# Summing seven groups' diagonal output quadrants in DRAM with accumulating DMAs instead of in SBUF with GpSimd additions

## The chip, the cores and the metric

The kernel runs on one core of one Trainium2 chip. The metric is the device time of one execution in microseconds (us). The engines are PE (matmuls, with weight loads listed as PEld), DVE (VectorE), ACT (ScalarE), POOL (GpSimd) and SP, which mostly issues DMAs; POOL and ACT can issue DMAs too.

## The reference

Linear attention is followed by a mixture of eight experts with dense routing. The first part makes `x`, 4608 rows of 512. Then, with `P` a 4608 x 8 table from a few rounds of row and column normalisation:

```
out = zeros((N, D))                  # 4608 x 512, float32
for e in range(E):                   # 8 experts
    h = maximum(x @ w1[e], 0)        # 4608 x 1024
    ye = h @ w2[e]                   # 4608 x 512
    out += P[:, e:e+1] * ye
```

The change concerns the last line alone: where the weighted contributions of the experts are added up.

## The kernel before

The 4608 rows are nine groups of 512: groups 0 to 7 are the first 512 tokens of the eight batches, group 8 collects the remaining 64 tokens of each. A running sum `acc[g]` of 128 partitions x 4 row tiles x 512 columns, float32, lies in SBUF for every group and is stored to `out` when expert 7 has been added.

After the attention and the routing, the experts 1 to 7 run as a long stream of matmuls. The up projection works on pairs of groups (0,1), (2,3), (4,5), (6,7), two halves (`fp`) for each pair, and on group 8 alone; in each of these nine steps the down projection of one earlier group is interleaved. Expert 7 takes group 8 first. Both projections are block products with seven instead of eight half-size products (a Strassen-Winograd scheme), and two of the up projection's products for a pair are split once more in the same way (`chain`, line 1487). The scheme needs sums of blocks: sums of the weights (`sums_up`, `sums_down`), of hidden blocks (`S[0]` to `S[2]` in `down7`), all made by `sub` on DVE (line 1223), and sums inside PSUM (line 1499, `ps<-ps,U`). The copies and relus of the up projection lie on ACT (lines 1455, 1459, 1467) and DVE (line 1462).

An output group falls into four quadrants (i, j): i is one half of its four row tiles, j is one half of its 512 columns. The down products `Z2`, `X2` and `X4` give the off-diagonal quadrants; `read` adds them to `acc` with two DVE instructions (line 1656). The products `Y1`, for quadrant (0,0), and `Z1` and `X3`, both for (1,1), give the diagonal ones by `read2`: two ACT instructions scale the PSUM bank by `P` into a buffer `u` (line 1668, seen as `hx<-ps,P` in the profile), and one POOL addition adds `u` to `acc` (line 1671). `u` comes from a ring `V` of two buffers. So there are three POOL additions for each group and expert from expert 1 on.

The weights of the next expert are loaded by POOL's DMA queue (`load_w`, line 500). From expert 2 on, the load names `("acc", 4, 0, 0)` among what it reads, so that it is held back until the running sum of group 4's first quadrant has last been written. Block sums of `x` come from DRAM on SP's queue (`load_x`, lines 1333 and 1341, tiles `XI` and `X`), in rings of two and three buffers that PE frees.

Nothing of the order is written by hand from instruction to instruction. A planner (`Plan`) takes every operation with a modelled duration, a queue, its reads and writes and its ring buffers, and runs a greedy list schedule: of all operations that are ready, the one that can start first goes first, and of equals the one that was emitted first. Each engine and queue then gets its instructions in the order of that schedule and executes them in that order. So taking away or adding an operation can change the order on every engine. POOL additions and DVE's `sub` are marked as shared: the planner lets only one of them run at a time.

Of the kernel before, what the change touches and what calls it, by code (L numbers as in the profile page):

```python
# [12 lines left out]
ALU = mybir.AluOpType  # L13
# [101 lines left out]

class Op:
    __slots__ = ("eng", "dur", "lat", "nbytes", "fn", "left", "ready", "users", "idx", "end",
                 "bufs", "deps", "shared", "turn", "unit", "stop", "tiled", "ins", "behind")

    def after(self, user):  # L120

# [77 lines left out]
class Plan:  # L199
# [9 lines left out]
    def op(self, eng, dur, lat, fn, r=(), w=(), takes=(), nbytes=0, shared=False):  # L209


        o = Op()
        o.eng, o.dur, o.lat, o.fn, o.nbytes = eng, dur, lat, fn, nbytes
        o.users, o.idx, o.end, o.ready = [], len(self.ops) + self.prio, None, 0.0
        o.shared, o.turn, o.unit, o.tiled = shared, False, 0, 0
        o.ins = o.behind = None
        deps = {}
        for key in r:
            for d in self.last.get(key, ()):
                deps[id(d)] = d  # L220
        for key in w:
            for d in list(self.last.get(key, ())) + self.readers.get(key, []):
                deps[id(d)] = d
        bufs = list(takes)
        for key in list(r) + list(w):
            b = key[0] if isinstance(key, tuple) else key
            if isinstance(b, Buf):
                bufs.append(b)
        o.bufs = list({id(b): b for b in bufs}.values())
        for b in o.bufs:  # L230
            b.left += 1
        for key in r:
            self.readers.setdefault(key, []).append(o)
        for key in w:
            self.last[key] = [o]
            self.readers[key] = []
        o.deps = list(deps.values())
        o.left = len(o.deps)
        for d in o.deps:
            d.users.append(o)  # L240
        self.ops.append(o)
        return o
# [81 lines left out]
    def run(self, tc):  # L324
        done = self.schedule()
        with tc.manual_schedule():
            for o in done:
                o.ins = o.fn()
                if o.behind:
                    tc.add_manual_dep(  # L330
                        o.ins.ins, o.behind.ins.ins.name, mybir.DependencyInfo(
                            mybir.DependencyClass.Sync, mybir.DependencyReason.DATA),
                        reason="order at the shared port")
# [3 lines left out]
def kernel(  # L337
# [151 lines left out]
    def new(tag):  # L489
        return R[tag].new()  # L490
# [914 lines left out]
    def up7(A, gs, fp, X, H, r0):  # L1405
# [155 lines left out]
            steps.update(chain("s1", w, A["s4"][1] + r0, hb, [("banks", 0, 0)], keep))  # L1561
        return steps

    def acc_part(g, i, j):
        return lambda: acc[g][:, 2 * i:2 * i + 2, 256 * j:256 * j + 256]

# [29 lines left out]
    def down7(e, g, H, B7):  # L1596


        def a(i, j):
            return lambda k: H[k // 2]()[:, j, k % 2, 256 * i:256 * i + 256]  # L1600

        def hk(i, j, fps=(0, 1)):
            return [(H[fp], q, j, i) for fp in fps for q in range(2)]

        late, seen = akey(g), set()
        S = [new(f"S{i}") for i in range(3)]
        for fp in range(2):
            def h(i, j, fp=fp):
                return lambda: H[fp]()[:, j, :, 256 * i:256 * i + 256]

            def s(n, fp=fp):
                return lambda: S[n]()[:, 2 * fp:2 * fp + 2]

            f = (fp,)
            end0 = ["dn0"] if e == 1 else []
            sub(dve, 512, s(0), h(1, 0), h(1, 1), ALU.add, hk(1, 0, f) + hk(1, 1, f) + end0,
                [(S[0], fp)])
            sub(dve, 512, h(1, 0), h(0, 0), h(1, 0), ALU.subtract, hk(0, 0, f), hk(1, 0, f))
            sub(dve, 512, s(1), s(0), h(0, 0), ALU.subtract,
                [(S[0], fp)] + hk(0, 0, f), [(S[1], fp)])  # L1620
            sub(dve, 512, s(2), h(0, 1), s(1), ALU.subtract,
                [(S[1], fp)] + hk(0, 1, f), [(S[2], fp)])

        def sk(n):
            return [(S[n], fp) for fp in range(2)]

        def sa(n):
            return lambda k: S[n]()[:, k, :]

        def prod(bank, lhs, y, r, first, more=(), wk=()):  # L1630
            f, r2 = B7[y]
            product(bank, lambda k, i: lhs(k)[:, 128 * i:128 * i + 128],
                    lambda k: f()[:, k, :], 4, r + r2 + (["P"] if e else late) + list(more), first,
                    wk=wk)

        def start(bank, i, j):

            out_ = acc_part(g, i, j)
            w = [("acc", g, 2 * i + n, j) for n in range(2)]
            if (i, j) in seen:  # L1640
                dve(515, lambda: nc.vector.tensor_tensor(
                    out=out_(), in0=bank().rearrange("p (a b) -> p a b", a=2), in1=out_(),
                    op=ALU.add), [bank] + late, w)
            else:
                act(512, lambda: nc.scalar.copy(
                    out=out_(), in_=bank().rearrange("p (a b) -> p a b", a=2)),
                    [bank] + late, w)
            seen.add((i, j))

        def read(bank, i, j):  # L1650

            if e == 0:
                return start(bank, i, j)
            for n in range(2):
                ts = 2 * i + n
                dve(320, lambda n=n, ts=ts: nc.vector.scalar_tensor_tensor(  # L1656
                    out=acc[g][:, ts, 256 * j:256 * j + 256],
                    in0=bank()[:, 256 * n:256 * n + 256], scalar=P[:, 4 * g + ts, e:e + 1],
                    in1=acc[g][:, ts, 256 * j:256 * j + 256], op0=ALU.mult, op1=ALU.add),
                    [bank, "P"], [("acc", g, ts, j)])  # L1660

        def read2(bank, i, j):

            if e == 0:
                return start(bank, i, j)
            u = new("V")
            for n in range(2):
                act(370, lambda n=n: nc.scalar.activation(  # L1668
                    out=u()[:, n, :], in_=bank()[:, 256 * n:256 * n + 256], func=ACT.Copy,
                    bias=0.0, scale=P[:, 4 * g + 2 * i + n, e:e + 1]), [bank, "P"], [(u, n)])  # L1670
            pool(695, lambda: nc.gpsimd.tensor_tensor(  # L1671
                out=acc[g][:, 2 * i:2 * i + 2, 256 * j:256 * j + 256],
                in0=acc[g][:, 2 * i:2 * i + 2, 256 * j:256 * j + 256], in1=u(), op=ALU.add),
                [(u, 0), (u, 1)], [("acc", g, 2 * i + n, j) for n in range(2)])

        if e == 1 and g < 9:
            for ts in range(4):
                act(670, lambda ts=ts: nc.scalar.activation(
                    out=acc[g][:, ts, :], in_=acc[g][:, ts, :], func=ACT.Copy, bias=0.0,
                    scale=P[:, 4 * g + ts, 0:1]), ["P", ("acc", g, ts), (H[0], 0, 1, 1)] + akey(g),  # L1680
                    [("acc", g, ts, j) for j in range(2)])
        x, y, z = new("P1"), new("PO"), new("P1")

        def X1():
            prod(x, a(0, 0), "11", hk(0, 0), True, sk(1) + hk(1, 0),
                 [("D", e, g)])
            act(512, lambda: nc.scalar.copy(out=y(), in_=x()), [x], [y])

        def Y1():
            prod(y, a(0, 1), "21", hk(0, 1), False, [("D", e, g)])  # L1690
            read2(y, 0, 0)

        def Z1():
            prod(z, sa(0), "t1", sk(0), True)
            read2(z, 1, 1)

        def X2():
            prod(x, sa(1), "t2", sk(1), False)
            read(x, 0, 1)

        def X3():
            prod(x, a(1, 0), "t3", hk(1, 0), False)
            read2(x, 1, 1)

        def Z2():
            prod(z, sa(2), "22", sk(2), False)
            read(z, 0, 1)

        def X4():
            prod(x, a(1, 1), "t4", hk(1, 1), False)  # L1710
            read(x, 1, 0)

        def stores():
            if e == E - 1 and g < 8:
                for ts in range(4):
                    store(g, ts)
            elif e == E - 1:
                held.extend(range(4))

        return {"out": stores, "X1": X1, "Y1": Y1, "Z1": Z1, "X2": X2, "X3": X3, "Z2": Z2, "X4": X4}  # L1720


# [26 lines left out]
    early, dn = [plain(8)], plain(7)  # L1749
    pairs = [(g, g + 1) for g in range(0, 8, 2)]  # L1750
    for e in range(1, E):
        w1, w2 = load_w(e, ["late", ("acc", 4, 0, 0)] if e > 1 else ["late"])
        if e == 1:
            nextX = sums_x(pairs[0])
# [67 lines left out]
```

## Time and the profile before

| what | value |
|---|---|
| time, three runs | 1013.84, 1014.08, 1014.84 us; median 1014.08 |
| span of the profiled execution | 1011.7 us |
| median less span (what lies around it) | 2.4 us |
| PE busy | 996.5 us, 99% |
| DVE, ACT, POOL busy | 84%, 79%, 38% |
| POOL additions of line 1671 | 186, 236.0 us in all |
| granted clock | 1.0 throughout |

Busy time of an engine counts its instructions as the profiler saw them. The chain that ended last follows the work back from the last instruction, at each step to what released it. A DMA's time to landing runs from its issue to the arrival of its data. The profiled execution's time is not listed apart from its span; the 2.4 us are the difference between the median and the span.

### The profile page before, as it was taken

What the parts mean: (1) busy time and instruction counts of PE and PEld (TensorE: products, weight loads), DVE (VectorE), ACT (ScalarE), POOL (GpSimd) and SP (SyncE); (2) the same over time, 40 slices, a digit from 0 to 9 for tenths busy, and PEclk for the clock granted to TensorE, in tenths of its full rate; (3) what the DMA queues carried; (4) which work ended last, traced back from release to release, by engine and by line L of the source; (5) the groups of instructions that cost most, each with busy time, mean ns of one, the idle gap of its engine ahead of it and who ended that gap; (6) DMA issues with size and microseconds to landing.
All of it is one profiled execution on the core that took longest, in us unless ns stands there. A gap on an engine that the chain in (4) does not pass through costs nothing.

```text
span 1011.7 us, 22473 instructions
## 1 busy us (share of the span) xinstructions
PE 996.5 (99%) x8195; PEld 713.6 (71%) x8232; DVE 851.8 (84%) x1979; ACT 797.0 (79%) x1786; POOL 379.7 (38%) x418
## 2 busy tenths in 40 slices
PE   7899999999999999999999999999999999999998
PEld 5666666644566867787777777787778777787775
DVE  8999989986888988789788988898778978888775
ACT  8999999836888787777777777768776877777774
POOL 5778764400133323342333323332333333433333
PEclk9999999999999999999999999999999999999999
DMA  9999989150114411171116121341126111612443
GB/s 253 198 191 177 166 148 134 38 115 1 48 48 96 114 48 48 48 138 56 48 48 117 48 57 52 73 93 48 48 51 144 48 48 48 110 53 69 154 154 142
DMA packets 115087, 93.94 MB, mean 93 GB/s; under 512 B 54432, under 2 KB 97440, under 8 KB 114976
## 3 DMA queue, kind: packets, MB, share of 16 engines
q1 hardware_dynamic: 83024, 68.46, 26.4%
q0 software_dynamic: 31648, 23.86, 17.0%
q8 instruction: 64, 1.05, 0.5%
q14 instruction: 47, 0.39, 0.1%
q10 hardware_dynamic: 304, 0.20, 0.1%
HBM read 92.62 MB, written 14.55 MB: 106 GB/s over the span
## 4 chain that ended last, share of the span: by engine, by line
PE 93%; ACT 3%; DVE 1%; DMA 1%; issue 1%; DVEq 0%
PE ps L1391 42%; PE ps L1400 25%; PE ps L605 17%; PE ps L1487 7%; PE ps L888 2%; ACT k L601 1%; ACT q L601 1%; DMA xT<-wx 1%; DVE wx L597 0%; PE ps L735 0%; DMA acc<-in_k_dram 0%; ACT wx L601 0%; PE ps L917 0%; ACT kr L601 0%; DVE m L597 0%
## 5 line engine op out<-in xcount | busy, mean ns | idle before, releaser
L1671 POOL TENSOR_TENSOR acc<-acc,hx 128x512 f32<-128x512 f32 x186 | 236.0, 1269 | 555.0 <-ACT hx L1668 287.5
L1391 PEld LDWEIGHTS <-hs 128*128 128x128 bf16 x1984 | 194.1, 98 | 56.2 <-issue 0.4
L1462 DVE CUSTOM_DVE_ANT_0 hs<-ps,U 128x512 bf16<-128x512 f32 x252 | 167.0, 685 | 46.6 <-PE ps L1400 29.0
L1668 ACT ACTIVATE hx<-ps,P 128x256 f32<-128x256 f32 x372 | 161.2, 482 | 45.2 <-PE ps L1391 42.3
L1467 ACT ACTIVATE hs<-ps 128x512 bf16<-128x512 f32 x252 | 151.1, 609 | 52.6 <-PE ps L1400 45.8
L1656 DVE SCALAR_TENSOR_TENSOR acc<-ps,P,acc 128x256 f32<-128x256 f32 x372 | 163.2, 476 | 31.8 <-PE ps L1391 30.7
L1391 PEld LDWEIGHTS <-hx 128*128 128x128 bf16 x1488 | 145.5, 98 | 27.1 <-issue 0.6
L1459 ACT COPY ps<-ps 128x512 f32<-128x512 f32 x252 | 146.4, 597 | 12.5 <-PE ps L1487 6.0
L1391 PE MATMUL ps<-hx,hs 128*128 128x256 bf16 x992 | 142.4, 273 | 0.1
L1400 PE MATMUL ps<-X,T 128*128 128x512 bf16 x448 | 131.5, 379 | 0.1
L1499 DVE TENSOR_TENSOR ps<-ps,U 128x256 f32<-128x256 f32 x192 | 75.5, 426 | 36.1 <-PE ps L1487 27.0
L1400 PEld LDWEIGHTS <-T 128*128 128x128 bf16 x672 | 65.7, 98 | 47.1 <-issue 0.6
L1455 ACT COPY U<-ps 128x512 f32<-128x512 f32 x126 | 74.7, 593 | 14.2 <-PE ps L1487 12.8
L1391 PE MATMUL ps<-wx,hs 128*128 128x256 bf16 x560 | 81.5, 273 | 0.0
L1391 PE MATMUL ps<-wx,hx 128*128 128x256 bf16 x496 | 75.9, 273 | 0.0
L1391 PE MATMUL ps<-hx 128*128 128x256 bf16 x496 | 75.9, 273 | 0.0
L1400 PE MATMUL ps<-xT,T 128*128 128x512 bf16 x224 | 72.5, 379 | 0.0
L605 PE MATMUL ps<-xT,w 128*128 128x512 bf16 x271 | 70.1, 379 | 0.6
L605 PE MATMUL ps<-w,hx 128*128 128x512 bf16 x274 | 69.7, 379 | 0.5
L1391 PE MATMUL ps<-w,hx 128*128 128x256 bf16 x432 | 69.8, 273 | 0.0
L1391 PE MATMUL ps<-w,hs 128*128 128x256 bf16 x432 | 64.7, 273 | 0.0
L597 DVE TENSOR_REDUCE m<-ps 128x4 f32<-128x512 f32 x88 | 58.7, 679 | 3.2 <-ACT k L601 1.5
(168 smaller groups left out, 1934.4 us busy)
## 6 DMA issues: line engine op xcount, KB each, us to landing
X<-xd SPq DMA_DIRECT2D x72, 256.0 KB, 2.7
wx<-in_moe_w_dram POOLq DMA_DIRECT2D x8, 1024.0 KB, 12.4
v_m<-in_v_dram SPq DMA_DIRECT2D x15, 512.0 KB, 5.7
out_dram<-acc SPq DMA_DIRECT2D x14, 512.0 KB, 3.2
w<-in_moe_w_dram POOLq DMA_DIRECT2D x6, 1024.0 KB, 10.8
XI<-xd SPq DMA_DIRECT2D x24, 192.0 KB, 2.5
qk<-in_k_dram POOLq DMA_DIRECT2D x12, 256.0 KB, 5.7
qk<-in_q_dram POOLq DMA_DIRECT2D x12, 256.0 KB, 6.9
```

What stands on the lines that cost most here:

```text
L605: nc.tensor.matmul(out_, lhsT=lhsT, rhs=rhs, start=start, stop=stop)
L1391: pe(256, lambda i=i, k=k, z=z: nc.tensor.matmul(bank()[:, 256 * i:256 * i + 256], lhsT=lhs(k, i), rhs=rhs(k), start=first and z, stop=k = ...
L1400: pe(512, lambda k=k: nc.tensor.matmul(bank().rearrange("p (a b) -> p a b", a=2), lhsT=lhs(k), rhs=rhs(k), start=first and k == 0, stop=k ...
L1455: act(512, lambda: nc.scalar.copy(out=u[q]().rearrange("p a b -> p (a b)"), in_=w[q]()), bk(w[q]), [u[q]])
L1459: act(512, lambda: nc.scalar.copy(out=to[q](), in_=x[q]()), bk(x[q]), [to[q]])
L1462: dve(515, lambda: nc.vector._custom_dve(ADD_SAT, out=out_(q, i, j), in0=bank[q]().rearrange("p (a b) -> p a b", a=2), in1=u[q](), s0=3.0e ...
L1467: act(512, lambda: nc.scalar.activation(out=out_(q, i, j), in_=bank[q]().rearrange("p (a b) -> p a b", a=2), func=ACT.Relu, bias=0.0, scal ...
L1487: pe(256, lambda: nc.tensor.matmul(at(i, h)(), lhsT=blocks[lhs]()[:, fp], rhs=rhs(), start=start, stop=True, skip_group_check=True), [*xal ...
L1499: dve(256, lambda: nc.vector.tensor_tensor(out=at(i, h)(), in0=at(1, 0)(), in1=s(), op=ALU.add), [k[1, 0], (p5, n)], [k[i, h]])
L1656: dve(320, lambda n=n, ts=ts: nc.vector.scalar_tensor_tensor(out=acc[g][:, ts, 256 * j:256 * j + 256], in0=bank()[:, 256 * n:256 * n + 256 ...
L1668: act(370, lambda n=n: nc.scalar.activation(out=u()[:, n, :], in_=bank()[:, 256 * n:256 * n + 256], func=ACT.Copy, bias=0.0, scale=P[:, 4 ...
L1671: pool(695, lambda: nc.gpsimd.tensor_tensor(out=acc[g][:, 2 * i:2 * i + 2, 256 * j:256 * j + 256], in0=acc[g][:, 2 * i:2 * i + 2, 256 * j: ...
```

## The change

For groups 0 to 6 (`NF = 7`), from expert 2 on, the diagonal quadrants are no longer added in SBUF.

- After expert 1, `sums()` stores the two diagonal quadrants of the group to `out` by two DMAs on SP's queue (256 KB each).
- From expert 2 on, `read2` scales the PSUM bank into a buffer `u` as before, but `u` comes from a new ring `VF` and is then added to `out` in DRAM by an accumulating DMA on POOL's queue (256 KB), instead of being added by POOL.
- `VF` has no memory of its own: its eight buffers are the diagonal quadrants of `acc[0]` to `acc[3]`, free once they are stored. An operation of no cost (`"X"`) holds the planner's first use until those eight stores have landed.
- Two operations that write the same quadrant of `out` get a real wait (`landed`): the accumulation of `X3` waits until that of `Z1` has landed, and the first one of each expert until the one of the expert before.
- At expert 7 the final stores of groups 0 to 6 hold only the off-diagonal quadrants (two of 256 KB a group in place of two of 512 KB).
- The key `("acc", 4, 0, 0)` that holds the weight loads back is no longer written for group 4 after expert 1.

Groups 7 and 8 and all of expert 1 keep the POOL additions.

```diff
+    def out_part(g, i, j):
+        return out[g * S:g * S + SM].rearrange("(p j) d -> p j d", j=NJ)[
+            :, 2 * i:2 * i + 2, 256 * j:256 * j + 256]
+
+    NF, NV, FAR = 7, 4, 320
+    R["VF"] = Ring(None, None, None, "VF", 0)
+    R["VF"].make = lambda n: acc_part(n // 2, n % 2, n % 2)()
+    R["VF"].free = [(0.0, n) for n in range(2 * NV)]
...
-            u = new("V")
+            u = new("VF" if far else "V")
             for n in range(2):
                 act(370, lambda n=n: nc.scalar.activation(
                     out=u()[:, n, :], in_=bank()[:, 256 * n:256 * n + 256], func=ACT.Copy,
-                    bias=0.0, scale=P[:, 4 * g + 2 * i + n, e:e + 1]), [bank, "P"], [(u, n)])
+                    bias=0.0, scale=P[:, 4 * g + 2 * i + n, e:e + 1]),
+                    [bank, "P"] + ["far"] * far, [(u, n)])
+            if far:
+                dma("POOL", 1 << 18, FAR, lambda: nc.gpsimd.dma_start(
+                    out=out_part(g, i, i), in_=u(), accum_op=ALU.add),
+                    [(u, 0), (u, 1)], [("far", g, i)])
+                return
             pool(695, lambda: nc.gpsimd.tensor_tensor(
...
+        far = e > 1 and g < NF
+
+        def sums():
+            if e == 1 and g < NF:
+                for i in range(2):
+                    dma("SP", 1 << 18, 320, lambda i=i: nc.sync.dma_start(
+                        out=out_part(g, i, i), in_=acc_part(g, i, i)()),
+                        [("acc", g, 2 * i + n, i) for n in range(2)], [("far", g, i)])
...
         def stores():
-            if e == E - 1 and g < 8:
+            sums()
+            if e == E - 1 and g < NF:
+                for i in range(2):
+                    dma("SP", 1 << 18, 320, lambda i=i: nc.sync.dma_start(
+                        out=out_part(g, i, 1 - i), in_=acc_part(g, i, 1 - i)()),
+                        [("acc", g, 2 * i + n, 1 - i) for n in range(2)], [("out", g, i)])
+            elif e == E - 1 and g < 8:
...
+        if e == 2:
+            plan.op("X", 0.0, 0.0, lambda: None, w=["far"], r=[("far", g, i) for g in range(NV)
+                                                               for i in range(2)])
```

More of the change, by code (lines that the diff above doesn't have):

```diff
@@ L117 @@
     __slots__ = ("eng", "dur", "lat", "nbytes", "fn", "left", "ready", "users", "idx", "end",
-                 "bufs", "deps", "shared", "turn", "unit", "stop", "tiled", "ins", "behind")
+                 "bufs", "deps", "shared", "turn", "unit", "stop", "tiled", "ins", "behind", "landed")
     def after(self, user):
@@ L216, in op @@
         o.ins = o.behind = None
+        o.landed = any(isinstance(key, tuple) and key[0] == "far" for key in w)
         deps = {}
@@ L328, in run @@
                 o.ins = o.fn()
+                for d in o.deps if o.landed else ():
+                    if d.landed:
+                        tc.add_manual_dep(
+                            o.ins.ins, d.ins.ins.name, mybir.DependencyInfo(
+                                mybir.DependencyClass.Sync, mybir.DependencyReason.DATA),
+                            reason="sums in DRAM")
                 if o.behind:
```

## The prediction

> **What bounds the kernel now.** I read the page's busy times and its chain of waits first, then PE's waits, the windows of single experts, the DVE groups kept apart by form, the DMA issues, and the timeline of the last 30 us. The page, first busy time and then the chain:
>
> ```profile
> PE 996.5 (99%) x8195; PEld 713.6 (71%) x8232; DVE 851.8 (84%) x1979; ACT 797.0 (79%) x1786; POOL 379.7 (38%) x418
> ...
> PE 93%; ACT 3%; DVE 1%; DMA 1%; issue 1%; DVEq 0%
> ```
>
> PE is the bound, and POOL, from which the change takes work, is the least loaded engine. A busy PE could still hide gaps, so I look at two whole experts (us, then busy us and instructions of PE, PEld, DVE, ACT, POOL, then clock, DMA share, GB/s):
>
> ```profile
> 441.34:549.27 107.93, 107.93 (x834) 81.38 (x833) 90.38 (x211) 83.12 (x185) 35.87 (x29) 1.00 0.29 68
> 549.27:657.21 107.94, 107.94 (x835) 81.37 (x833) 90.42 (x211) 83.13 (x185) 35.88 (x29) 1.00 0.30 68
> ```
>
> and at the chain in order of time:
>
> ```profile
> 441.34 17.03 PE ps L1391 x156
> ...
> 549.27 17.03 PE ps L1391 x156
> ```
>
> 156 narrow matmuls (256 columns) in 17.03 us are 0.109 us each; ten wide ones (512 columns, line 1400) take 2.16 us there, 0.216 each. The program has 160 wide and 672 narrow matmuls per expert: 34.6 + 73.3 = 107.9 us, the period itself. So there is no hidden gap, and PE's waits after 310 us are empty in the trace. Nothing that speeds POOL, DVE or ACT can shorten an expert; the change can only add waits, or change the end.
>
> DVE by form, 370 to 1005 us (count, busy us, mean ns, idle before):
>
> ```profile
> L1223 DVE TENSOR_TENSOR hx<-hs,hx 128x512 bf16<-128x512 bf16 x106 | 51.8, 494 | 0.2
> L1223 DVE TENSOR_TENSOR hs<-hs 128x512 bf16<-128x512 bf16 x105 | 46.9, 446 | 1.5
> L1223 DVE TENSOR_TENSOR hx<-hx,hs 128x512 bf16<-128x512 bf16 x105 | 46.0, 438 | 0.0
> L1223 DVE TENSOR_TENSOR hx<-hs 128x512 bf16<-128x512 bf16 x105 | 42.9, 415 | 1.1 <-PE ps L1391 1.0
> ...
> L1223 DVE TENSOR_TENSOR hx<-w,hx 128x1024 bf16<-128x1024 bf16 x3 | 2.1, 684 | 0.0
> ```
>
> DVE has 90.4 of each 107.9 us busy: over a few us it is as tight as PE. That matters below.
>
> **Part 1, work removed.** 6 experts x 7 groups x 3 = 126 of POOL's 186 additions go; at the row's 1269 ns that is 160 us of POOL time. PE waits for none of them: worth nothing. The two ACT scalings before each stay.
>
> **Part 2, work added on POOL's queue.** 126 accumulating DMAs of 256 KB, 21 an expert. POOL's own 256 KB loads hold it 0.585 to 0.815 us, so about 17 us an expert against the 27 us that leave. The trace has no accumulating transfer. Nearest rows for issue to landing, L (KB, us):
>
> ```profile
> X<-xd SPq DMA_DIRECT2D x72, 256.0 KB, 2.7
> wx<-in_moe_w_dram POOLq DMA_DIRECT2D x8, 1024.0 KB, 12.4
> ...
> w<-in_moe_w_dram POOLq DMA_DIRECT2D x8, 256.0 KB, 5.5
> ```
>
> From below 2.7 us, from above 12.4 us for four times the elements; I take 5.5, same queue and same size. In a step of 108/9 = 12.0 us POOL must issue three, and `X3`'s waits at the head of the queue until `Z1`'s has landed. Behind it stand the other accumulations, the weight loads and the additions of groups 7 and 8. The queue keeps up while L + 2 x 0.8 stays under 12.0, so L up to 10.4; eight buffers cover more than two steps of lag before ACT, and then PE's banks, wait. At 5.5 the cost is nil.
>
> **Part 3, DMA traffic.** 5.5 MB more an expert is 51 GB/s written, and as much read, beside the 68 above. The `XI` and `X` loads are what it could delay: they are issued from 471.2 us on and first read from 480.5 us, 9 to 11 us later, and their slowest landing in that expert is 7.2 us, beside weight loads. Nothing, up to another 2 us a load. The weight loads lose their hold and start when their ring frees, some 85 us before use. The 14 early stores stand on SP in expert 1, ahead of stores of `X` that nothing needs soon. Nil.
>
> **Part 4, the order.** This decides. The built programs have the same 16333 rows on PE, but from the middle of expert 1 the order differs on PE, DVE and ACT, because the planner schedules with other constraints. Step costs come from the timeline, as distances of instructions in a row: line 1462 0.645 us (two in 1.29), a pair of line 1656 0.88, a block sum of 512 0.41 and of 1024 0.68, line 1499 0.43.
>
> ```profile
> 991.29 1.29 DVE L1462 CUSTOM_DVE_ANT_0 hs<-ps,U 128x512 bf16<-128x512 f32 x2 [1.04 <-PE ps L1400]
> ...
> 1003.80 0.88 DVE L1656 SCALAR_TENSOR_TENSOR acc<-ps,P,acc 128x256 f32<-128x256 f32 x2 [0.93 <-PE ps L1391]
> ```
>
> In experts 3 to 6, at the second half of the first pair, PE needs the first addition in PSUM (line 1499). In both orders DVE does one of the last weight sums just before it. Before: line 1462, four sums of 512, a weight sum, a pair, then the addition: 0.645 + 1.64 + 0.68 + 0.88 + 0.43 = 4.28 us, while PE has 39 narrow and 2 wide matmuls queued, 4.68 us: 0.4 to spare. After: line 1462, one sum of 512, the weight sum, the pair, the addition: 3.05 us, but PE has only 15 narrow and 2 wide, 2.07 us. Taken from the product that starts this DVE run (line 1462, weight sum, line 1462, pair, and then the above), it is 5.9 us of DVE against 20 narrow and 8 wide matmuls, 3.9 us. PE waits 2.0 us, four times: 8.0. In expert 2 a weight sum of `w2` waits for PE to leave a `TB` buffer, and the block sum that PE needs next stands behind it and a pair: 0.68 + 0.88 + 0.41, less one matmul: 1.9. `Y1` follows `X1` there with 0.44 us of matmuls under ACT's 0.59 us copy: 0.15 five times, 0.7. One ACT run early in expert 2 (copy 0.59, pair of scalings 0.84, over 0.76 us of matmuls): 0.7. Sum 11.3 us. Bounds: none of it, if DVE runs ahead at these places; twice, 23, if each handover costs and each wait pushes the next instructions back. I take the count itself.
>
> **Part 5, the end.** `Z1` and `X3` of group 6 now end in DRAM:
>
> ```profile
> 1000.38 0.84 ACT L1668 ACTIVATE hx<-ps,P 128x256 f32<-128x256 f32 x2 [0.89 <-PE ps L1391]
> ...
> 1008.65 0.33 SPq L1187 DMA_DIRECT2D out_dram<-acc  x1
> ```
>
> `Z1` is scaled at 1001.2; two landings in a row at 5.5 end at 1012.2, against the span's 1011.7: +0.5 us (nil at 2.7; +3 at 6.9, the slowest POOL row of that size; +14 at 12.4). The Trainium skill (DMA: Bandwidth & Descriptors, Anatomy of one DMA) gives a DMA from GpSimd about 2.0 us plus its bytes at 436 GB/s, an estimate of 2.6 us here: by it the end would cost nothing. The 2.7 of SP's row agrees, POOL's 5.5 does not.
>
> **Sum.** The profiled span 1011.7 + 11.3 + 0.5 = 1023.5; what lies around the span is 2.4 us, median less span, so 1025.9. I say **1026**.
>
> **Rivals.**
> - *The waits are swallowed.* DVE reaches those places earlier than the count says, since it loses its delays from POOL; PE stays full. For it: the spare need only grow by 2 us. Against it: both runs start from a PE product, which DVE can't get ahead of. 1014 to 1017, say 1015. Chance 0.12.
> - *Faster, since DVE gets rid of POOL.* The three slow forms above exceed 415 ns by 8.4 + 3.3 + 2.4 = 14 us, with single ones near 990; with four fifths of the additions gone, 11 us return, 1.8 an expert. This decides if PE waits on DVE. Then 1014.1 - 11 = 1003. Against it: the two periods are full of matmuls, so the wait isn't there. Chance 0.04. The Trainium skill (SBUF — State Buffer, Who interferes with whom) has DVE's instructions with two SBUF inputs and GpSimd's reads lock each other out of a shared port; the 990 against 415 ns agree.
> - *Accumulation is slow.* If L is above 10.4, POOL's queue is the bound and each of 42 steps grows by the excess: at 12.4, 1026 + 42 x 2.0 = 1110. For it: read, add and write may take several times a copy. Against: 256 KB loads with a conversion land in 5.5. Chance 0.14.
> - That the change doesn't do what it says is excluded: the built order has 126 accumulations and 60 additions.
>
> **Numbers.** Forecast 0.70, own range 1018 to 1036 (half the count to twice, with the end). No change means within 0.2%, about 2 us, what a measurement can tell. Swallowed waits give 0.08 to same, 0.04 to slower. Faster 0.04. Slower 0.70 + 0.14 + 0.04 = 0.88. The range 1015 to 1050 leaves out faster, some of same and most of slow accumulation.
>
> **What would show it.** Right: PE waits on DVE near the start of experts 3 to 6, periods near 110 us, in expert 2 a wait on a sum of line 1230, landing of the accumulations at 4 to 7 us, POOL busy well below 38%. Wrong: periods of 107.9 us, or POOL's queue waiting on its own landings step after step.

## The result, and the profile after

The changed kernel takes **1031.59 us** (median of four runs: 1030.06, 1030.38, 1032.79, 1032.80) against 1014.21 for the kernel before in the same session: a ratio of 1.0166, 95% interval 1.0143 to 1.0189. The profiled execution has a span of 1031.0 us, 19.3 more than before; it is one of the two longer runs (1032.80).

The page first, with the lines that matter here: busy times, the chain, the two forms of POOL's work and the DMA issues.

```profile
PE 1001.4 (97%) x8195; PEld 713.1 (69%) x8232; DVE 845.0 (82%) x1979; ACT 800.0 (78%) x1786; POOL 372.7 (36%) x418
...
PE 88%; DVE 3%; ACT 3%; DMA 3%; issue 1%; SPq 1%; POOLq 0%; DVEq 0%; ACTq 0%
...
L1689 POOL DMA_DIRECT2D out_dram<-acc x126 | 152.2, 1275 | 349.9 <-ACT acc L1684 305.5
...
L1693 POOL TENSOR_TENSOR acc<-acc,hx 128x512 f32<-128x512 f32 x60 | 76.1, 1270 | 212.8 <-ACT hx L1684 134.5
...
out_dram<-acc POOLq DMA_DIRECT2D x126, 256.0 KB, 4.7
X<-xd SPq DMA_DIRECT2D x72, 256.0 KB, 2.9
```

PE's share of the chain falls from 93% to 88%: something now keeps it from working without a pause. POOL is hardly relieved: each accumulating DMA holds it 1275 ns in the mean, as long as the addition it replaced (1269). A landing takes 4.7 us. The loads of `X` land in 2.9 us instead of 2.7, so the added traffic delays them little.

The chain in order of time shows the period of one expert by the long row of narrow matmuls that each of these experts has once:

```profile
448.37 16.48 PE ps L1398 x151
...
558.70 16.48 PE ps L1398 x151
...
669.01 16.48 PE ps L1398 x151
...
779.05 16.48 PE ps L1398 x151
```

The distances are 110.3, 110.3 and 110.0 us, where they were 107.9. PE's waits after 310 us, an empty list before, are now (waiter, what it waited for: us in all, times, the longest):

```profile
PE ps L1494 <- DVE ps L1506: 2.9, 5, 0.7
PE ps L1398 <- DVE acc L1672: 1.6, 1, 1.6
PE ps L1494 <- ACT U L1503: 1.2, 4, 0.3
PE ps L1494 <- ACT hx L1684: 0.9, 4, 0.2
PE ps L1398 <- ACT hx L1684: 0.4, 1, 0.4
PE ps L1407 <- DVE hs L1469: 0.2, 1, 0.2
```

No line says POOL or DMA: PE waits for DVE and ACT. Nor is it the clock: from 42 to 1023 us the granted clock is 1.00. The list adds up to less than PE loses, because the ends of matmuls are modelled; the starts of PE's matmuls, which are recorded, give the loss itself. So I split each span in three: up to the first matmul that reads `XI` (expert 1, ahead of the first accumulation), from there to the start of PE's last matmul, and the end behind that.

| us | first `XI` matmul | last matmul starts | between | end behind it |
|---|---|---|---|---|
| before | 351.48 | 1007.83 | 656.35 | 3.89 |
| after | 354.24 | 1023.47 | 669.23 | 7.54 |
| difference | 2.76 | 15.64 | 12.88 | 3.65 |

The 2.76 us come from the attention stage, which the change doesn't touch. PE's waits of that stage name a load, for 2.1 us, that the profile of before doesn't have among them (`rT` is a tile of that stage), and from near the end of that wait the granted clock is 0.50 for 3.4 us:

```profile
PE ps L612 <- DMA rT<-qk_r: 2.1, 1, 2.1
```

Two of the four runs are 2.5 us shorter than the other two, which would fit this wait coming and going, but only one of the four is profiled; in the kernels below, the first `XI` matmul starts between 350.80 and 352.91. What belongs to the change is 12.88 + 3.65 = 16.5 us, and with 1014.2 that is 1030.7, 0.3 to 0.7 us above the shorter pair. The median of 1031.59 holds some 0.9 us more than that.

The end, from the timeline (start, us, what, idle before) and the chain:

```profile
1017.10 1.20 POOL L1689 DMA_DIRECT2D out_dram<-acc  x1 [0.49 <-ACT acc L1684]
...
1023.37 1.20 POOL L1689 DMA_DIRECT2D out_dram<-acc  x1 [5.07 <-DMA out_dram<-acc]
...
1024.29 0.34 SPq L1194 DMA_DIRECT2D out_dram<-acc  x1
```

```profile
1016.34 0.47 ACT acc L1684
1016.81 0.29 issue
1017.10 5.73 DMA out_dram<-acc
1022.83 0.02 issue
1022.85 0.02 POOLq L1689
1022.87 0.47 issue
1023.35 1.23 POOLq L1857
```

`Z1`'s accumulation lands at 1022.83; only then is `X3`'s issued, and the span ends behind its landing. Before, the last plain store (then at 1008.65) ended the span 3.1 us later.

### The profile page after: what moved, and what is told of

Same layout as the page of the kernel before. It is cut to its first block, busy times and chain, and to the rows that moved or that the text cites. A ratio compares the mean times of both kernels' runs of the same rounds, so it can differ in the third digit from the quotient of the medians.

```text
span 1031.0 us, 22476 instructions
## 1 busy us (share of the span) xinstructions
PE 1001.4 (97%) x8195; PEld 713.1 (69%) x8232; DVE 845.0 (82%) x1979; ACT 800.0 (78%) x1786; POOL 372.7 (36%) x418
## 3 DMA queue, kind: packets, MB, share of 16 engines
HBM read 92.62 MB, written 47.58 MB: 136 GB/s over the span
## 4 chain that ended last, share of the span: by engine, by line
PE 88%; DVE 3%; ACT 3%; DMA 3%; issue 1%; SPq 1%; POOLq 0%; DVEq 0%; ACTq 0%
PE ps L1398 39%; PE ps L1407 23%; PE ps L612 16%; PE ps L1494 7%; PE ps L895 2%; DVE hs L1469 1%; DMA rT<-qk_r 1%; DVE hx L1230 1%; DMA xT<-wx 1%; DVE acc L1672 1%; DMA acc<-in_q_dram 1%; ACT q L608 1%; DMA out_dram<-acc 1%; ACT k L608 0%; ACT hs L1474 0%
## 5 line engine op out<-in xcount | busy, mean ns | idle before, releaser
L1689 POOL DMA_DIRECT2D out_dram<-acc x126 | 152.2, 1275 | 349.9 <-ACT acc L1684 305.5
L1469 DVE CUSTOM_DVE_ANT_0 hs<-ps,U 128x512 bf16<-128x512 f32 x252 | 167.5, 686 | 52.8 <-PE ps L1407 38.6
L1672 DVE SCALAR_TENSOR_TENSOR acc<-ps,P,acc 128x256 f32<-128x256 f32 x372 | 163.1, 477 | 38.3 <-PE ps L1398 36.8
L1693 POOL TENSOR_TENSOR acc<-acc,hx 128x512 f32<-128x512 f32 x60 | 76.1, 1270 | 212.8 <-ACT hx L1684 134.5
L1684 ACT ACTIVATE acc<-ps,P 128x256 f32<-128x256 f32 x252 | 107.2, 484 | 20.6 <-PE ps L1398 19.3
L1506 DVE TENSOR_TENSOR ps<-ps,U 128x256 f32<-128x256 f32 x192 | 76.4, 428 | 41.3 <-PE ps L1494 31.4
L1398 PE MATMUL ps<-hx 128*128 128x256 bf16 x496 | 73.7, 272 | 0.7
```

What stands on the lines that cost most here:

```text
L1398: pe(256, lambda i=i, k=k, z=z: nc.tensor.matmul(bank()[:, 256 * i:256 * i + 256], lhsT=lhs(k, i), rhs=rhs(k), start=first and z, stop=k = ...
L1469: dve(515, lambda: nc.vector._custom_dve(ADD_SAT, out=out_(q, i, j), in0=bank[q]().rearrange("p (a b) -> p a b", a=2), in1=u[q](), s0=3.0e ...
L1506: dve(256, lambda: nc.vector.tensor_tensor(out=at(i, h)(), in0=at(1, 0)(), in1=s(), op=ALU.add), [k[1, 0], (p5, n)], [k[i, h]])
L1672: dve(320, lambda n=n, ts=ts: nc.vector.scalar_tensor_tensor(out=acc[g][:, ts, 256 * j:256 * j + 256], in0=bank()[:, 256 * n:256 * n + 256 ...
L1684: act(370, lambda n=n: nc.scalar.activation(out=u()[:, n, :], in_=bank()[:, 256 * n:256 * n + 256], func=ACT.Copy, bias=0.0, scale=P[:, 4 ...
L1689: dma("POOL", 1 << 18, FAR, lambda: nc.gpsimd.dma_start(out=out_part(g, i, i), in_=u(), accum_op=ALU.add), [(u, 0), (u, 1)], [("far", g, i)])
```

## The experiments

**Theory**: the transfers cost PE nothing inside the experts; the new order of PE, DVE and ACT makes the 12.9 us, and two landings in a row make the 3.65 us. **Rivals**: the accumulating transfers themselves (bytes, POOL's queue), or one of them colliding with the weight loads.

All kernels are measured against the kernel before on the same chip (median 1013.5 to 1014.2); "between" and "end" are the columns of the table above, as differences from before.

| kernel | median us | ratio, interval | between | end |
|---|---|---|---|---|
| after | 1031.59 | 1.0166 [1.0143, 1.0189] | +12.9 | +3.65 |
| e1, old order | 1045.55 | 1.0310 [1.0291, 1.0329] | +25.8 | +4.2 |
| e2, old order, six groups | 1026.36 | 1.0123 [1.0108, 1.0138] | +12.4 | +0.3 |
| e3, new order, POOL additions | 1042.68 | 1.0278 [1.0260, 1.0295] | +28.2 | +0.2 |
| e4, new order, plain stores | 1027.42 (one run) | | +12.9 | 0.0 |
| e5, old order, `X3` apart | 1016.08 | 1.0023 [1.0014, 1.0032] | -0.3 | +0.9 |
| e6, new order, no sums | 1027.00 | 1.0127 [1.0112, 1.0142] | +13.2 | +0.1 |
| e7, last `X3` apart | 1027.53 | 1.0135 [1.0120, 1.0150] | +13.7 | +0.8 |
| e8, four groups | 1013.72 | 0.9995 [0.9985, 1.0004] | -0.3 | 0.0 |
| e10, loads held | 1024.83 | 1.0103 [1.0087, 1.0120] | +7.2 | +3.5 |
| e11, five groups | 1022.64 | 1.0082 [1.0067, 1.0097] | +8.3 | -0.2 |
| e9, loads held, DMA cost 250 | 1018.34 | 1.0055 [1.0038, 1.0072] | +0.3 | +3.2 |

**e1 and e2: the change's transfers in the order of before.** The schedule is planned with the POOL addition; the DMA is issued in its place.

```diff
-            pool(695, lambda: nc.gpsimd.tensor_tensor(... op=ALU.add),
+            def add():
+                if far:
+                    behind_landing(nc.gpsimd.dma_start(
+                        out=out_part(g, i, i), in_=part(), accum_op=ALU.add), (g, i))
...
+            pool(695, add,
```

> The change's transfers (126 accumulating DMAs, the early stores, the halved final stores, eight buffers in the diagonal quadrants) in the order of instructions that the kernel before has: the planner plans POOL additions as before, and only what is emitted differs, so PE and DVE have the same instruction order as before. Theory 'order' (the waits of PE come from the new order, the transfers themselves cost only the end): about 1018 us, that is 1014.2 plus the 3.7 us at the end, periods of an expert 107.9 us, no wait of PE between 340 us and the last group. Theory 'transfers' (accumulating DMAs, their descriptors or their traffic hold up ACT, DVE or PE): 1027 to 1031 us, with periods near 110 us as in the changed kernel.

> As the kernel with the old order and the change's transfers, but group 6 keeps the POOL additions in SBUF (six groups, not seven, are summed in DRAM), so that no accumulation stands near the end. If the end's cost is the two landings in a row of group 6's quadrant (1,1): 1014 us, within 1 us of the kernel before, and 3 to 4 us less than with seven groups. If the end costs because of traffic or the queue's backlog: 1016 to 1018 us.

Neither time came. PE and DVE run in the order of before, and e1 is still 14 us slower than the changed kernel. Its waits of PE, and then ACT's on POOL:

```profile
PE ps L1394 <- ACT U L1458: 16.4, 4, 4.6
```

```profile
ACT hx L1708 <- POOL acc L1698: 20.6, 5, 5.4
```

So PE waits for ACT, ACT for an addition of POOL (its buffer isn't free). PE's four waits cost more than their own length: near the end of each the granted clock falls to 0.50 for 3.4 to 6.8 us, and PE's wide matmuls start 0.43 us apart instead of 0.216. By the starts of the matmuls the waits are 17.1 us and the slow stretches 7.2 us of the 25.8. POOL's timeline tells why ACT waits:

```profile
431.57 2.20 POOL L500 DMA_DIRECT2D wx<-in_moe_w_dram  x2
438.10 1.21 POOL L1695 DMA_DIRECT2D out_dram<-acc  x1 [4.33 <-ACT acc L1708]
452.44 3.67 POOL L1695 DMA_DIRECT2D out_dram<-acc  x3 [13.12 <-DMA X<-xd]
461.41 2.43 POOL L1695 DMA_DIRECT2D out_dram<-acc  x2 [5.30 <-ACT hx L1708]
462.90 3.65 POOL L1698 TENSOR_TENSOR acc<-acc,hx 128x512 f32<-128x512 f32 x2
```

The two weight loads (1 MB each) stand right ahead of `Z1`'s accumulation at 438.10, which lands after 13.8 us instead of 5. `X3`'s accumulation waits for that landing at the head of POOL's queue, and what stands behind it waits too, the additions of groups 7 and 8 among it. (The bracket names another transfer; but `Z1`'s landing, 438.10 + 13.8, is 0.54 us ahead of the next issue, the same 0.54 us as at the end of the changed kernel.) e2 loses 12.4 us; ACT's waits on POOL's additions are 16.0 us there, but PE's are shorter (at most 2.0 us) and the clock stays at 1.00 inside the experts. Why it comes off so much better with one group less is not shown. The end alone came out as expected: +0.3 us without group 6 against +4.2.

**e5: the same order, without the wait for the landing.** `X3`'s addend goes to a DRAM tensor of its own.

```diff
-                        out=out_part(g, i, i), in_=part(), accum_op=ALU.add), (g, i))
+                        out=other[g] if second else out_part(g, i, i), in_=part(),
+                        accum_op=ALU.add), (g, i, second))
```

> The kernel of e1 (the order of before on TensorE and VectorE, the transfers of the change for groups 0 to 6), but X3's accumulation of each group goes to a DRAM tensor of its own, so that it has no landing of Z1's accumulation to wait for; that addend is left out of the output. Theory 1, collision in POOL's queue: the 31.5 us of e1 come from X3's DMA waiting at the head of POOL's in-order queue for Z1's landing, which the weight loads delay, with the SBUF additions of groups 7 and 8 late behind it. Then PE's four waits of 4.6 us on ACT and ACT's waits on POOL are gone, and the time is 1014 to 1019. Theory 2, accumulating transfers themselves (their bytes, or POOL's 1.2 us in each) slow the rest: as many of them, as heavy as before, so 1040 to 1046.

1016.08, and "between" is back at before's value. The landings next to the weight loads are as slow as ever (up to 16.4 us), and there are as many accumulations of the same size; but no accumulation waits for them, and inside the experts the clock stays at 1.00:

```profile
433.38 2.21 POOL L500 DMA_DIRECT2D wx<-in_moe_w_dram  x2
439.94 1.21 POOL L1698 DMA_DIRECT2D out_dram<-acc  x1 [4.34 <-ACT acc L1714]
440.67 1.61 POOL L1698 DMA_DIRECT2D other<-acc  x1
444.58 1.19 POOL L1698 DMA_DIRECT2D out_dram<-acc  x1 [2.29 <-ACT acc L1714]
```

So e1's loss is the wait at the head of the queue, with what follows from it, and not the transfers. In the order of before, 126 accumulating DMAs are free inside the experts as long as none waits for another's landing.

**e3: the new order with additions in place of the DMAs.**

```diff
-                dma("POOL", 1 << 18, FAR, lambda: nc.gpsimd.dma_start(
-                    out=out_part(g, i, i), in_=u(), accum_op=ALU.add),
+                dma("POOL", 1 << 18, FAR, lambda: nc.gpsimd.tensor_tensor(
+                    out=acc_part(g, i, i)(), in0=acc_part(g, i, i)(), in1=u(), op=ALU.add),
```

> The reverse: the changed kernel's order on PE, DVE and ACT, but each accumulating DMA is a POOL addition into SBUF again (buffers: the two of ring V; no early stores; full final stores). Theory 'order': 1027 us (1025 to 1029), the same waits of PE near the start of experts 3 to 6, each period 110 us, expert 2 longest, and an end like before's. Theory 'transfers': 1014 us.

1042.68 lies outside both. It is not a clean test: the eight buffers shrink to two, ACT waits 13.7 us for POOL's additions, a wait that the changed kernel doesn't have, and DVE is busy 870 us against 845. PE's waits on L1503 are after's, 1.2 us; those on DVE are larger. It settles nothing, and e6 takes its place.

**e4: plain stores**, `accum_op` left out of all 126.

> The changed kernel with plain stores in place of accumulations (accum_op left out; the summation over experts of these quadrants is left out with it). If adding in DRAM is what makes a transfer slow: landing falls from 4.7 us to 3.5 or less, POOL is held 0.8 us instead of 1.2 for each, and the end is 2 to 3 us shorter; if the rows of 1 KB and the queue do: 4.7 and 1.2 us stay. The waits of PE at the start of each expert stay in either case by theory 'order'.

PE's waits are after's to a tenth of a microsecond, "between" is +12.9 again, and the end's 3.65 us are gone, more than the 2 to 3 expected. What accumulating costs shows in POOL's group and in the landing:

```profile
L1689 POOL DMA_DIRECT2D out_dram<-acc x126 | 91.4, 726 | 400.3 <-ACT acc L1684 374.8
...
out_dram<-acc POOLq DMA_DIRECT2D x126, 256.0 KB, 2.6
```

Accumulating 256 KB holds POOL 0.55 us longer (1275 against 726 ns) and lands 2.1 us later (4.7 against 2.6). The Trainium skill (DMA: Bandwidth & Descriptors, Anatomy of one DMA) gives the estimate of 2.6 us for this size from GpSimd: the plain store agrees with its 2.6, the accumulating one takes 4.7.

**e6: the new order, with neither DMA nor addition** for the quadrants that the change sums in DRAM; ACT's scalings stay.

```diff
-                dma("POOL", 1 << 18, FAR, lambda: nc.gpsimd.dma_start(
-                    out=out_part(g, i, i), in_=u(), accum_op=ALU.add),
+                dma("POOL", 1 << 18, FAR, lambda: None,
```

> The changed kernel with its own order on PE, DVE and ACT, but with neither an accumulating DMA nor an addition for the diagonal quadrants from expert 2 on: ACT's scalings stay, their sums are left out. Theory 1, order: PE's waits of experts 2 to 6 (12.9 us in the profile of after) stand in the order itself and stay, PE's wait lines keep 0.7 us on the block sums per expert 3 to 6, and only the end (3.6 us) is saved: 1026 to 1028. Theory 2, transfers and POOL's work cause the waits: 1013 to 1016. Between the two: the order leaves PE no slack, and POOL's DMA work makes part of the delay, 1018 to 1024.

1027.00, with 126 of POOL's instructions gone and these waits of PE (the four largest):

```profile
PE ps L1494 <- DVE ps L1506: 2.8, 5, 0.7
PE ps L1398 <- DVE acc L1672: 1.6, 1, 1.6
PE ps L1494 <- ACT U L1503: 1.2, 4, 0.3
PE ps L1494 <- ACT hx L1684: 0.8, 4, 0.2
```

The waits are the changed kernel's without its transfers. The order makes all of the 12.9 us.

**e7: the last `X3` accumulation alone** goes to a tensor of its own.

```diff
+        ALONE.append(nc.gpsimd.dma_start(out=other, in_=u, accum_op=ALU.add))
...
+                dma("POOL", 1 << 18, FAR, lambda: last_part(u()) if last else nc.gpsimd.dma_start(
```

> The changed kernel, but the very last accumulation (X3 of group 6 in expert 7) goes to a DRAM tensor of its own and has no landing of Z1's to wait for; that addend is left out of the output. Theory 1, the end is one landing waited for and a second one behind it: X3 is issued some 5 us earlier, lands before the last plain store, which then ends the span about 3.0 us after its issue as in before; 3.0 to 4.0 us less than after, 1026.3 to 1028.8 by the median. Theory 2, the end is late because what stands ahead of it is late, and the landing only shows it: no change, 1030 to 1033.

1027.53; the end falls from 7.5 to 4.7 us behind the last matmul, by 2.8, a little less than expected. The second landing, waited for, is most of the end.

**e8 and e11: four and five groups** (`NF = 4`, `NF = 5`).

> The changed kernel with the quadrants of groups 0 to 3 alone summed in DRAM (NF = 4, 48 accumulations instead of 84 in the seven groups' experts 2 to 7, and groups 4 to 8 in SBUF as before). The weight loads' key, the first sum of group 4, is then again written in every expert, and the planner's order stands close to that of before. Theory 1, the order and the weight loads' lost hold make the loss and the accumulation is free: 1013.5 to 1016. Theory 2, each accumulation costs a share of the 12.9 us of experts 2 to 6: 48 of 84 give 7.4 us, 1020 to 1023.

> The changed kernel with groups 0 to 4 summed in DRAM (NF = 5): one group more than e8, and that group writes the key of the weight loads. Theory 1, losing that key is what spoils the order: PE's waits come back in experts 2 to 6 at 6 to 13 us in all, with no accumulation at the very end (group 6 is in SBUF): 1019 to 1027. Theory 2, the loss grows with the number of groups alone: one group more than none lost at four, 1014 to 1018.

The expectation of e8 miscounts: it is 72 accumulations of 126, the same share. At four groups the kernel is as fast as before, PE has no wait after 310 us, and the 72 accumulations are free. At five, with the key of the weight loads lost, 8.3 us are back. That fits the lost key as cause, but doesn't show it alone, since the planner's whole order changes with it.

**e10 and e9: the hold on the weight loads put back**, then one constant of the planner besides (an accumulating DMA costed at 250 ns on POOL, not 320).

```diff
-        w1, w2 = load_w(e, ["late", ("acc", 4, 0, 0)] if e > 1 else ["late"])
+        w1, w2 = load_w(e, ["late", ("far", 4, 0)] if e > 2 else ["late", ("acc", 4, 0, 0)] if e > 1
+                         else ["late"])
...
-    NF, NV, FAR = 7, 4, 320
+    NF, NV, FAR = 7, 4, 250
```

> The changed kernel with the weight loads held again: in experts 3 to 7 they wait in the planner for the first DRAM sum of group 4, as they waited in before for its first SBUF sum; the planner orders everything anew. Theory 1, lost hold alone: the order waits shrink towards before and only the end is left, 1017 to 1022. Theory 2, hold and landing collide: on POOL the two weight loads stand again right ahead of the accumulations of groups 4 and 5, as in e1, X3 waits some 13 us for Z1's landing behind their bytes, and the waits of ACT on POOL and of PE on ACT come back: 1030 to 1050. Theory 3, the hold has nothing to do with it: 1029 to 1033.

> The kernel of e10 (the changed kernel with the weight loads held again), with one constant of the planner more: it takes 250 ns, not 320, for an accumulating DMA on POOL; all 126 accumulations and all arithmetic stay as in the changed kernel, only the order that the planner finds is another. Theory 1, what is left in e10 beside the end (some 7 us) is order again and nothing that the transfers do: if this order is better, PE's waits shrink towards none and the end's 3.6 us alone are left, 1016 to 1020. Theory 2, what is left in e10 is the price of 126 accumulations beside PE's work, whatever the order: 1023.5 to 1026.

The hold alone brings "between" from 12.9 to 7.2 us, so it falls between its theories. That fits the lost hold as a part of the cause, but doesn't show it, since the planner orders everything anew here too. The collision of e1 doesn't return: ACT has no wait on POOL. With the constant, which changes nothing on the chip but the order, all seven groups summed in DRAM cost 0.3 us inside the experts, with POOL's work as heavy as in the changed kernel:

```profile
L1689 POOL DMA_DIRECT2D out_dram<-acc x126 | 152.2, 1260 | 341.4 <-ACT acc L1684 277.0
```

and all of PE's waits after 310 us are

```profile
PE ps L1407 <- DVE hs L1469: 0.2, 1, 0.2
```

though accumulations next to the weight loads land as late as 14.2 us: the planner, which knows of the wait, puts other accumulations between `Z1`'s and `X3`'s. What is left is the end, 3.2 us (the median, 4.8 us above before's, is 1.3 more than the two columns add up to; its four runs spread over 2.8 us). No version here beats the kernel before, and with PE full inside the experts none of this kind can; e8 equals it.

## Why the prediction was right, and which term was off

The forecast was 1026, slower, in 1015 to 1050; it came out at 1031.59, in the range and in its direction, and by the mechanism given: PE waits at the foreseen places because of the order. In size it forecast 11.8 us for the change, and the change itself cost 16.5; most of the difference is one term, the end. (The sum also took 2.4 us for what lies around the span, the median of before less the span of another run. Every run that is listed with its own span is 1.8 us longer than it, so before's profiled execution was some 0.6 us faster than the median.)

- **Part 1 and 3, POOL's additions and the traffic, nil: right.** Neither removing the additions nor adding the bytes moved PE: e6 without transfers has the same "between" as after (+13.2, +12.9), and e5, the old order without the additions, that of before (-0.3). The "as much read" of Part 3 is not seen: the pages count 33.0 MB more written to DRAM (14.55 to 47.58) and no more read (92.62 in both).
- **Part 2, POOL's queue, nil: right in this order, with a wrong price.** I took 0.585 to 0.815 us of POOL per DMA from its loads; it is 1.2. So POOL's busy time fell to 36%, not "well below 38%". Landing was 4.7 us in the median against the 5.5 taken from a load; beside weight loads eight took 9.5 to 11.7 us. The queue kept up, but e1 shows that this hangs on the order: next to weight loads a landing takes 12 to 16 us, above the limit of 10.4 worked out there, and then the queue does stop PE.
- **Part 4, the order, 11.3 us: measured 12.9.** The DVE run that was counted at 5.9 us stands on the chain, in expert 3:

```profile
483.21 0.69 DVE hs L1469
483.90 0.60 DVE hx L1230
484.50 0.59 DVE hs L1469
485.09 0.31 issue
485.41 0.48 DVE acc L1672
485.88 0.60 DVE hs L1469
486.48 0.93 DVE hx L1230 x2
487.41 0.58 DVE acc L1672 x2
487.99 0.13 issue
488.12 0.43 DVE ps L1506
488.55 0.04 issue
488.59 0.60 PE ps L1494 x4
```

  It is the same list of instructions, 5.3 us long, and PE's product follows its end. Each of the experts 3 to 6 loses about 2.0 us here (the gaps between starts of matmuls are 0.38 + 0.47 + 0.83 + 0.30), as forecast, but in four pieces, of which only one is the wait on L1506; the forecast had a single wait. That the size came to 2.0 is partly luck. The prediction's step costs are durations, not distances: from start to start the relu of line 1462 (now L1469), the weight sum, the pair and the sum of 512 are 0.60, 0.60, 0.79 and 0.33 us in this run, where it took 0.645, 0.68, 0.88 and 0.41, so the run was priced 0.6 us too long. In return it left out 0.3 us ahead of the run (the matmuls of its first product have been issued by 482.9, and DVE starts at 483.21, which the chain puts down to a relu of ACT), and the last 0.30 of the four pieces, which by the chain waits for a copy of ACT (line 1718) behind the run. Expert 2 lost about 4.5 us against 3.3 counted, 1.6 to 1.7 of it at the place foreseen, though the profile names the pair (`acc L1672`) and not the block sum as the last to come. (The 16333 rows of PE in Part 4 stand in no page, which count 8195 + 8232; nothing rests on them.)
- **Part 5, the end, +0.5: measured +3.65. This is the mis-sized term.** The two landings came to the size taken (5.73 and 5.2 us; 10.9 against 11.0), with some luck, since the 5.5 was the row of a load and the median of the 126 is 4.7. The working set the second landing against the end of the span and left out what lies around the two: 0.29 us from scaling to issue, 0.54 from the first landing to the next issue, and 2.46 from the last landing to the end of the span: 3.3 us. The bound of the unknown landing held this size, the value did not. By the estimate of the Trainium skill (DMA: Bandwidth & Descriptors, Anatomy of one DMA), 2.6 us a landing, it would have been nil, which was further off.
- **Rivals.** "Swallowed waits" did not happen. "Faster by DVE relief": DVE did get time back, some 8 us of the 11 reckoned, on its four forms of 512 (421 sums in 187.6 us before and 419 in 178.6 after, between 370 and 1005 us; the slowest form from 494 to 440 ns), and none of it reached PE, as argued. "Slow accumulation" did not come in the changed kernel, but its mechanism, `X3` waiting at the head of POOL's queue for a landing above 10.4 us, is e1's, there at places beside the weight loads.

## What to carry to other kernels

Where the bound engine has no gap and its helper is 84% busy, a change that only moves work between idle units is decided by what it does to the order: count the instructions of the helper between two that the bound engine needs, in the built order of both versions. Price the last transfers of a kernel from the last compute instruction to the end of the span, with every issue and the tail behind the landing, not landing by landing. And where a DMA waits for another's landing at the head of an in-order queue, look at what else the DMA engines carry just then.

## What the runs showed of the hardware

- An accumulating DMA of 256 KB into DRAM landed in 4.7 us against 2.6 for a plain store of the same data on the same queue, and held POOL 1275 against 726 ns, as long as the addition of 128x512 that it replaced (1269 ns).
- Behind two weight loads of 1 MB on the same queue such a DMA landed in 12.3 to 14.2 us (e9), up to 16.4 in e5, and PE lost nothing by it: in e5 no accumulation waited for it, and in e9 the waits for a landing at the head of POOL's queue stayed short (none above 3.4 us before the end, against 13.1 and 13.4 in e1).
- A wait of PE can cost more than its length: near the end of each of e1's four waits of 4 to 4.7 us the granted clock fell to 0.50 for 3.4 to 6.8 us, 7.2 us in all. In the changed kernel's attention stage the same happened for 3.4 us with a wait of 2.1 us.
- POOL's additions slow DVE's block sums: in the kernel before, each DVE sum of 128x512 that took over 900 ns (23 behind 370 us, against 415 ns for the fastest form's mean) ran while a POOL addition ran; in the changed kernel two such long sums are left, both beside a POOL addition.
- In the attention stage a wait on the load of `rT` was absent, 1.3 or 2.1 us from run to run (before, e9, after), in a part that no edit touched. Differences of 2 us between single profiles have to be placed before they are explained.
